# Second mixture: another order of the seven block products, copies ahead of casts on ScalarE, input forms over two rounds

## The chip, the cores and the metric

The kernel runs on one core of a Trainium2 chip. The time is the device time of one execution in microseconds (us), the median of the runs. PE is the matrix engine (TensorE), ACT is ScalarE, DVE is VectorE, POOL is GpSimd, SP issues the weight loads. Each engine works through a stream of instructions of its own, and semaphores order them against each other.

## What is computed

Attention over a window of 128 keys (4 batches, 8 heads, 576 positions), then a mixture of 8 experts with one expert for each token, then the second mixture, which this change is about: 4 experts on all 2304 tokens, weighted by given probabilities.

```python
def _moe2_ref(x, domain_probs, w1, w2):          # x 2304x512, w1 4x512x1024, w2 4x1024x512
    p = domain_probs / (domain_probs.sum(-1, keepdims=True) + 1e-09)
    out = np.zeros((N, D), dtype=np.float32)
    for e in range(E):
        h = np.maximum(x @ w1[e], 0.0)
        out += p[:, e:e + 1] * (h @ w2[e])
    return out
```

## The kernel before

Every fp32 matrix is carried as two fp32r tiles, an upper one (a cast on ACT) and a lower one (what the cast left, a subtraction on DVE); a product is three matmuls (upper by upper, upper by lower, lower by upper). The order of all instructions is written out by hand: each engine works through its own instructions in the order in which the program names them.

The second mixture runs 24 units, `unit2(u)`: 3 passes over the tokens (768 tokens each, two chunks of 384), 4 experts each, 2 rounds each (half of the hidden columns). So units 0, 8 and 16 are the first of a pass, units 7, 15 and 23 the last.

**Layer 1 of a unit** multiplies a 2x2 block matrix of the weights by one of the inputs with seven block products instead of eight. The inputs' seven *forms* are made once in a pass by `x_forms`, a generator that makes one form for each `next`: `b11`, `b21` and `b22` are plain blocks (one cast on ACT, one subtraction on DVE), `t1` to `t4` are differences (one subtraction `less` on DVE ahead of that). A product goes into two PSUM banks, twelve matmuls in all, by `step(banks, weight form, input form, start)`. There are three pairs of banks. `X` goes on accumulating over four products (a11, s2, s3, a22), and its sums on the way are needed: `keep` copies the two X banks on ACT after a11 (`m1`), after s2 (`u2`) and after s3 (`u3`). The next product into X may start only when the bank has been copied. `join` adds a copy to a bank of Y or Z on DVE and makes the upper half of the hidden tile with a Relu on ACT; `low` makes its lower half on DVE. The order of the products before: X a11, Z s1, X s2, X s3, Y a12, X a22, Z s4.

**Layer 2** has six accumulations (`n` = 0 to 5) of twelve matmuls, two banks of `ps_g` and one of `ps_t` in turn; `gather` adds each to the output rows on DVE (`acc`, line 1137). The last unit of a pass stores each row tile with an indirect DMA issued on POOL.

Between the steps `between(...)` advances generators: `ahead` prepares weight tiles (a tile of w2 is one 1024-wide cast on ACT and one subtraction `wlo` on DVE; a tile of w1 has its mixed forms besides), two advances in layer 1 (the w2 tiles of this same unit, here called item 2 and item 3) and four in layer 2 (items 0 and 1 of the next unit). `opening` is `x_forms(0)` in unit 0, where two forms had been made before; `closing` is `x_forms(p + 1)` in the last unit of a pass, which makes all seven forms of the next pass, three in layer 1 and four in layer 2.

Of the kernel before, what the change touches and what calls it, by code (L numbers as in the profile page):

```python
# [26 lines left out]
E1, E2 = 8, 4  # L27
# [3 lines left out]
NPASS = NCHUNK // 2  # L31
# [16 lines left out]
def kernel(  # L48
# [582 lines left out]
    def moe():  # L631
        mctx = ExitStack()
        with mctx:
# [15 lines left out]
            def form(n, name):  # L649
                pool = xp if n < 2 * NDT else late_forms[0]  # L650
                return pool.tile([P, 2, CH], F32R, tag=f"f{n}", name=name)
# [35 lines left out]
            def x_forms(p):  # L687
                l, r = (slice((2 * p + k) * CH, (2 * p + k + 1) * CH) for k in range(2))
                (b11, b12), (b21, b22) = ((x2[j][:, :, l], x2[j][:, :, r]) for j in range(2))
                now = ready[p] = {}  # L690

                temp = x2[0][:, :, N:]

                def split(n, k, src):
                    hi, lo = (form(2 * n + i, f"{k}{'hl'[i]}{p}") for i in range(2))
                    nc.scalar.copy(out=hi, in_=src)
                    nc.vector.tensor_tensor(out=lo, in0=src, in1=hi.bitcast(F32), op=ALU.subtract)
                    now[k] = hi, lo

                def less(out, a, b):  # L700
                    nc.vector.tensor_tensor(out=out, in0=a, in1=b, op=ALU.subtract)  # L701

                split(0, "b11", b11)
                yield
                less(temp, b12, b11)
                split(1, "t1", temp)
                yield
                less(temp, b22, temp)
                split(2, "t2", temp)
                yield  # L710
                less(b12, b22, b12)
                split(3, "t3", b12)
                yield
                split(4, "b21", b21)
                yield
                less(temp, b21, temp)
                split(5, "t4", temp)
                yield
                split(6, "b22", b22)
                yield  # L720

            def first_mixture():
                pctx = ExitStack()
                with pctx:
# [257 lines left out]
                    for _ in post:  # L982
                        pass

            forms = x_forms(0)

            def early(n):
# [18 lines left out]
            accs = {}  # L1006
            rounds = [(p, e, r) for p in range(NPASS) for e in range(E2) for r in range(2)]

            def unit2(u):
                p, e, r = rounds[u]  # L1010
                opening = forms if u == 0 else iter(())
                closing = x_forms(p + 1) if (e, r) == (E2 - 1, 1) and p + 1 < NPASS else iter(())
                w0 = n_first + ROUND * u
                xf = ready[p]
                at = {
                    "a11": (0, 0), "a12": (0, Q), "a22": (0, 2 * Q), "s3": (0, 3 * Q),
                    "s1": (2, 0), "s2": (2, Q), "s4": (2, 2 * Q),
                }

                def product(ps, n, a, b, start):  # L1020
                    tile0, c0 = at[a]
                    whi, wlo = wts[n][tile0:tile0 + 2]
                    xhi, xlo = xf[b]
                    for kt in range(2):
                        for x, (wl, xl) in enumerate(((whi, xhi), (whi, xlo), (wlo, xhi))):
                            nc.tensor.matmul(  # L1026
                                ps, wl[:, c0 + kt * P:c0 + (kt + 1) * P], xl[:, kt, :],
                                start=(start and kt == 0 and x == 0), stop=(kt == 1 and x == 2),
                                skip_group_check=not start,
                            )  # L1030

                def bank(tag, nm):
                    pool = {"a": ps_a, "g": ps_g, "t": ps_t}[tag]
                    return pool.tile([P, CH], F32, tag=tag, name=nm)

                xb, yb = ([bank("a", f"{k}{u}_{i}") for i in range(2)] for k in "XY")
                zb = [bank("g", f"Z{u}_{i}") for i in range(2)]
                hs = {}
                snaps = {}

                def keep(k, i):
                    if u == 0:
                        to = yp.tile([P, DM], F32, tag="y", name=f"{k}_{i}")[:, 0:CH]
                    else:
                        j, d = {"m1": (0, 1), "u2": (1, 0), "u3": (1, 1)}[k]
                        to = x2[j][:, d, (2 * p + i) * CH:(2 * p + i + 1) * CH]
                    nc.scalar.copy(out=to, in_=xb[i])  # L1047
                    snaps[k, i] = to

                def join(key, k, ps):  # L1050
                    hi = hp_.tile([P, CH], F32R, tag="hhi", name="hhi")
                    lo = hp_.tile([P, CH], F32R, tag="hlo", name="hlo")
                    c = ps
                    if k is not None:
                        c = sums[k[1]]
                        nc.vector.tensor_tensor(out=c, in0=ps, in1=snaps.pop(k), op=ALU.add)  # L1056
                    nc.scalar.activation(out=hi, in_=c, func=AF.Relu)  # L1057
                    hs[key] = hi, lo, c

                def low(key):  # L1060
                    hi, lo, c = hs[key]
                    nc.vector.scalar_tensor_tensor(  # L1062
                        out=lo, in0=c, scalar=0.0, in1=hi.bitcast(F32), op0=ALU.max, op1=ALU.subtract
                    )

                def step(bs, a, b, start):
                    for i in range(2):
                        product(bs[i], w0 + i, a, b, start)

                def between(*more):  # L1070
                    next(opening, None)
                    for todo in more:
                        next(todo, None)

                step(xb, "a11", "b11", True)
                between(ahead)
                for i in range(2):
                    keep("m1", i)
                step(zb, "s1", "t1", True)
                between(ahead, closing)  # L1080
                step(xb, "s2", "t2", False)
                between(closing)
                for i in range(2):
                    keep("u2", i)
                step(xb, "s3", "t3", False)
                between(closing)
                for i in range(2):
                    keep("u3", i)
                for i in range(2):
                    join((1, 1, i), ("u3", i), zb[i])  # L1090
                step(yb, "a12", "b21", True)
                between()
                for i in range(2):
                    low((1, 1, i))
                for i in range(2):
                    join((0, 0, i), ("m1", i), yb[i])
                step(xb, "a22", "t4", False)
                for i in range(2):
                    low((0, 0, i))
                for i in range(2):  # L1100
                    join((1, 0, i), None, xb[i])
                step(zb, "s4", "b22", False)
                for i in range(2):
                    low((1, 0, i))
                for i in range(2):
                    join((0, 1, i), ("u2", i), zb[i])
                for i in range(2):
                    low((0, 1, i))

                for n in range(2 * TT):  # L1110
                    k, t = divmod(n, TT)
                    acc = (ps_g, ps_t)[n % 2].tile([P, DM], F32, tag="gt"[n % 2], name="l2")
                    ts = slice(t * P, (t + 1) * P)
                    order = [(h, i) for h in ((0, 1), (1, 0))[k] for i in range(2)]
                    for m, (h, i) in enumerate(order):
                        whi, wlo = wts[w0 + 2 + h]
                        hhi, hlo, _ = hs[h, k, i]
                        c0 = i * DM
                        for x, (hl, wl) in enumerate(((hhi, whi), (hhi, wlo), (hlo, whi))):
                            nc.tensor.matmul(  # L1120
                                acc, hl[:, ts], wl[:, c0:c0 + DM],
                                start=(m == 0 and x == 0), stop=(m == 3 and x == 2),
                            )
                    if n < 4:
                        next(ahead, None)
                    if n > 1:
                        next(closing, None)
                    gather(p, e, r, n, acc)

# [19 lines left out]
    with tc.manual_schedule():  # L1149
        attention()  # L1150
        moe()
# [58 lines left out]
```

## Time and profile before

| | |
|---|---|
| three runs | 1201.73, 1202.87, 1203.39 us; median 1202.87 |
| the profiled execution | 1197.88 us; span from first to last instruction 1196.2 us |
| PE, ACT, DVE busy | 1167.6, 517.7, 785.6 us of the span |
| second mixture | from 431.8 us to the end |

Most of the second mixture is PE work without gaps, so what is to be looked for is how long single units last, and where PE sat idle in the longer ones. A row of the timeline gives the start of an instruction, its duration, engine and line, the tiles that it writes and reads, and in brackets the idle time of its engine ahead of it with what ended that.

### The profile page before, as it was taken

To read this page: it belongs to the slowest core of one execution; us is meant where nothing else is said; L and a number is where in the kernel's file an instruction comes from. 1 tells how busy PE (TensorE), PEld (TensorE's weight loads), DVE (VectorE), ACT (ScalarE), POOL (GpSimd) and SP (SyncE) were. 2 spreads that over 40 slices of the span, in tenths; PEclk is the share of its full clock that TensorE was granted. 3 is DMA by queue.
4 is the path that set the end of the run, shared out by engine and by line. 5 is a ranking of instruction groups with operands and counts; after the bars stand their busy time and mean duration, and the time that the engine had idled before them with its cause. 6 is when DMAs were issued, how large, how long until landed. Compare 5 with 4: busy or idle time off the path is not lost.

```text
span 1196.2 us, 18240 instructions
## 1 busy us (share of the span) xinstructions
PE 1167.6 (98%) x7006; PEld 1061.4 (89%) x7006; DVE 785.6 (66%) x1434; ACT 517.7 (43%) x926; POOL 94.7 (8%) x127
## 2 busy tenths in 40 slices
PE   8999998999999999999999899999999999999997
PEld 6888877999999988999999799999998899999996
DVE  6878764555565467666667876666667766666663
ACT  4565542454454344333334444443334433333331
POOL 8300110012200000000000110000000200000001
PEclk9999999999999999999999999999999999999999
DMA  9755424464574322222222222222221322222201
GB/s 315 262 163 188 142 63 155 143 200 141 159 221 149 124 72 71 71 71 71 65 63 67 89 88 69 57 69 71 71 65 58 124 72 71 71 71 71 71 19 53
DMA packets 62232, 126.67 MB, mean 106 GB/s; under 512 B 26272, under 2 KB 26272, under 8 KB 62112
## 3 DMA queue, kind: packets, MB, share of 16 engines
q1 hardware_dynamic: 58368, 114.96, 30.7%
q0 software_dynamic: 3456, 9.51, 2.1%
q8 instruction: 83, 1.36, 0.5%
q10 hardware_dynamic: 288, 0.52, 0.1%
q14 instruction: 37, 0.30, 0.1%
HBM read 109.18 MB, written 15.80 MB: 104 GB/s over the span
## 4 chain that ended last, share of the span: by engine, by line
issue 42%; PE 37%; DVE 2%; POOL 2%; ACT 1%; POOLq 0%; ACTq 0%; DVEq 0%
PE g L679 10%; PE l L1120 9%; PE y L786 8%; PE X L1026 4%; PE Z L1026 2%; POOL out_dram L1141 2%; PE y L797 1%; PE Y L1026 1%; PE xps L742 1%; DVE hlo L1062 1%; DVE x L701 0%; ACT hhi L1057 0%; DVE x L1056 0%; ACT whi L126 0%; PE g L767 0%
## 5 line engine op out<-in xcount | busy, mean ns | idle before, releaser
L130 DVE TENSOR_TENSOR wlo<-raw,whi 128x1024 fp32r<-128x1024 f32 x160 | 195.0, 1221 | 113.4 <-ACT whi L126 113.3
L1120 PE MATMUL l<-whi,hhi 128*128 128x512 f32 x576 | 225.4, 391 | 4.3 <-DVE acc L1137 4.0
L126 ACT CAST whi<-raw 128x1024 fp32r<-128x1024 f32 x160 | 168.3, 1057 | 134.1 <-DVE raw L152 104.6
L1120 PE MATMUL l<-whi,hlo 128*128 128x512 f32 x576 | 225.6, 392 | 0.0
L1120 PE MATMUL l<-wlo,hhi 128*128 128x512 f32 x576 | 225.3, 391 | 0.0
L1047 ACT COPY x<-X 128x384 f32<-128x384 f32 x138 | 65.8, 480 | 237.7 <-PE X L1026 237.7
L1137 DVE SCALAR_TENSOR_TENSOR acc<-l,ct,acc 128x512 f32<-128x512 f32 x126 | 94.3, 749 | 82.2 <-PE l L1120 82.2
L1120 PEld LDWEIGHTS l<-whi,hhi 128*128 128x128 f32 x576 | 108.6, 189 | 27.5 <-DVE acc L1137 4.8
L1120 PEld LDWEIGHTS l<-whi,hlo 128*128 128x128 f32 x576 | 108.5, 188 | 22.9 <-DVE hlo L1062 0.3
L1120 PEld LDWEIGHTS l<-wlo,hhi 128*128 128x128 f32 x576 | 108.6, 189 | 22.0
L1057 ACT ACTIVATE hhi<-x 128x384 fp32r<-128x384 f32 x144 | 74.1, 526 | 75.0 <-DVE x L1056 75.0
L1056 DVE TENSOR_TENSOR x<-Z,x 128x384 f32<-128x384 f32 x92 | 50.8, 556 | 81.9 <-ACT x L1047 72.9
L1141 POOL DMA_INDIRECT out_dram<-acc,ctok x18 | 23.0, 1276 | 842.9 <-DVE acc L1137 493.2
L1062 DVE SCALAR_TENSOR_TENSOR hlo<-x,hhi 128x384 fp32r<-128x384 f32 x144 | 77.4, 554 | 11.5 <-ACT hhi L1057 7.5
L400 ACT ACTIVATE pr<-sc,nm 128x256 f32<-128x256 f32 (+1 forms) x144 | 58.9, 464 | 52.4 <-DVE nm L392 24.6
L426 PE MATMUL xo<-vr,ptr 128*128 128x73 f32 x544 | 69.0, 279 | 0.6 <-ACT ptr L413 0.5
L786 PE MATMUL y<-hhi,whi 128*128 128x256 f32 (+2 forms) x224 | 69.5, 310 | 0.0
L786 PE MATMUL y<-hhi,wlo 128*128 128x256 f32 (+2 forms) x224 | 69.1, 308 | 0.0
L786 PE MATMUL y<-hlo,whi 128*128 128x256 f32 (+2 forms) x224 | 68.9, 308 | 0.0
L426 PEld LDWEIGHTS xo<-vr,ptr 128*128 128x128 f32 x544 | 63.7, 192 | 5.8 <-ACT ptr L413 1.3
L667 DVE SCALAR_TENSOR_TENSOR hlo<-g,hhi 128x384 fp32r<-128x384 f32 x64 | 32.7, 552 | 29.8 <-ACT hhi L666 29.5
L666 ACT ACTIVATE hhi<-g 128x384 fp32r<-128x384 f32 x64 | 28.0, 489 | 54.5 <-PE g L767 41.7
(337 smaller groups left out, 2546.4 us busy)
## 6 DMA issues: line engine op xcount, KB each, us to landing
raw<-in_w_b_dram SPq DMA_DIRECT2D x96, 512.0 KB, 3.5
raw<-in_w_a_dram SPq DMA_DIRECT2D x64, 512.0 KB, 4.1
xs<-zrow SPq DMA_DIRECT2D x8, 768.0 KB, 6.9
row<-xs SPq DMA_DIRECT2D x7, 768.0 KB, 5.6
rk<-in_k_dram SPq DMA_DIRECT2D x18, 256.0 KB, 4.9
vr<-in_v_dram SPq DMA_DIRECT2D x18, 256.0 KB, 3.9
rv<-in_vt_dram SPq DMA_DIRECT2D x18, 256.0 KB, 3.4
rq<-in_q_dram SPq DMA_DIRECT2D x16, 256.0 KB, 5.2
```

The source lines that it names most:

```text
L126: nc.scalar.copy(out=hi, in_=src)
L130: nc.vector.tensor_tensor(out=lo, in0=src, in1=hi.bitcast(F32), op=ALU.subtract)
L400: nc.scalar.activation(out=pr[:, r, jj, 0:w], in_=sc[s][:, r, jj, 0:w], func=AF.Exp, bias=nm[:, r, jj:jj + 1], scale=1.0,)
L426: nc.tensor.matmul(xo[:, 2 * jj + r, :], pt[:, r, c, :], vr[:, keys[c] % NSLOT, h, :], start=(c == 0), stop=(c == nk - 1),)
L679: nc.tensor.matmul(ps[:, 0:w], wl[:, c0:c0 + P], xl[dt // 2][:, dt % 2, 0:w], start=(n == 0), stop=(n == 3 * NDT - 1),)
L786: nc.tensor.matmul(acc[:, 0:w], wl[:, c0:c0 + P], hl[:, 0:w], start=(f == 0 and x == 0), stop=(f == NFT - 1 and x == 2),)
L1026: nc.tensor.matmul(ps, wl[:, c0 + kt * P:c0 + (kt + 1) * P], xl[:, kt, :], start=(start and kt == 0 and x == 0), stop=(kt == 1 and x == 2) ...
L1047: nc.scalar.copy(out=to, in_=xb[i])
L1057: nc.scalar.activation(out=hi, in_=c, func=AF.Relu)
L1062: nc.vector.scalar_tensor_tensor(out=lo, in0=c, scalar=0.0, in1=hi.bitcast(F32), op0=ALU.max, op1=ALU.subtract)
L1120: nc.tensor.matmul(acc, hl[:, ts], wl[:, c0:c0 + DM], start=(m == 0 and x == 0), stop=(m == 3 and x == 2),)
L1137: nc.vector.scalar_tensor_tensor(out=accs[g], in0=acc, scalar=pe, in1=accs[g], op0=ALU.mult, op1=ALU.add)
```

## The change

- **Order of the products.** After: X a11, Z s1, Y a12, X s2, X s3, X a22, Z s4. Y a12 stands two steps earlier, and X s2, s3 and a22 follow each other directly.
- **Copies ahead of casts.** `keep("m1")` is issued ahead of `between(ahead)`, no longer behind it. Behind X s2 and X s3 no `between` stands any more; the copies are issued right behind their products. The join of the block (0, 0), from Y and `m1`, is issued behind Y a12, that is ahead of the copies of `u2`.
- **Forms over two rounds.** `b21` is made third instead of fifth. The last unit of a pass makes five forms of the next pass (two in layer 1, three in layer 2, at `n` = 2, 4, 5) and leaves `t4` and `b22` to the first unit of the next pass, which makes them in its first two `between`. Unit 0 makes `b21` and `t2` ahead of its first product, and `t3`, `t4`, `b22` in its three `between`.
- **Where copies go.** The first unit of every pass, not only unit 0, keeps its copies in the pool `yp`, in which the output rows live too.

```diff
 def x_forms(p):
                 split(1, "t1", temp)
                 yield
+                split(2, "b21", b21)
+                yield
                 less(temp, b22, temp)
-                split(2, "t2", temp)
+                split(3, "t2", temp)
                 yield
                 less(b12, b22, b12)
-                split(3, "t3", b12)
-                yield
-                split(4, "b21", b21)
+                split(4, "t3", b12)
                 yield
...
+            border = {0: forms}
+
             def unit2(u):
                 p, e, r = rounds[u]
-                opening = forms if u == 0 else iter(())
-                closing = x_forms(p + 1) if (e, r) == (E2 - 1, 1) and p + 1 < NPASS else iter(())
+                fresh = (e, r) == (0, 0)
+                opening = border.pop(p) if fresh else iter(())
+                closing = iter(())
+                if (e, r) == (E2 - 1, 1) and p + 1 < NPASS:
+                    closing = border[p + 1] = x_forms(p + 1)
...
                 def keep(k, i):
-                    if u == 0:
+                    if fresh:
...
+                def pair(do, *a):                    # do(*a, i) for i in 0, 1
+                def joined(h, k, kept, bs):          # join for i in 0, 1
+                def lows(h, k):                      # low for i in 0, 1
+                if u == 0:
+                    next(opening)
+                    next(opening)
                 step(xb, "a11", "b11", True)
+                pair(keep, "m1")
                 between(ahead)
-                for i in range(2):
-                    keep("m1", i)
                 step(zb, "s1", "t1", True)
                 between(ahead, closing)
+                step(yb, "a12", "b21", True)
+                joined(0, 0, "m1", yb)
+                between(closing)
                 step(xb, "s2", "t2", False)
-                between(closing)
-                for i in range(2):
-                    keep("u2", i)
+                pair(keep, "u2")
+                lows(0, 0)
                 step(xb, "s3", "t3", False)
-                between(closing)
-                for i in range(2):
-                    keep("u3", i)
-                for i in range(2):
-                    join((1, 1, i), ("u3", i), zb[i])
-                step(yb, "a12", "b21", True)
-                between()
-                for i in range(2):
-                    low((1, 1, i))
-                for i in range(2):
-                    join((0, 0, i), ("m1", i), yb[i])
+                pair(keep, "u3")
+                joined(1, 1, "u3", zb)
                 step(xb, "a22", "t4", False)
-                for i in range(2):
-                    low((0, 0, i))
-                for i in range(2):
-                    join((1, 0, i), None, xb[i])
+                lows(1, 1)
+                joined(1, 0, None, xb)
                 step(zb, "s4", "b22", False)
...
-                    if n > 1:
+                    if n in (2, 4, 5):
                         next(closing, None)
                     gather(p, e, r, n, acc)
```

## Rows read from the trace of the kernel before

**Rows 1.** Busy time of each engine in units 0, 4, 7, 8, 15.

```profile
core 0: us, PE busy (x) PEld busy (x) DVE busy (x) ACT busy (x) POOL busy (x), PEclk, DMA share, GB/s
431.79:466.62 34.83, 32.08 (x159) 27.88 (x158) 26.99 (x41) 16.85 (x27) 0.00 (x0) 1.00 0.22 73
...
559.46:590.40 30.94, 30.94 (x157) 28.11 (x156) 20.72 (x34) 12.16 (x20) 0.00 (x0) 1.00 0.23 68
652.30:689.10 36.80, 33.12 (x157) 29.15 (x156) 30.33 (x45) 17.17 (x27) 6.11 (x5) 0.95 0.27 86
689.10:720.05 30.95, 30.95 (x158) 28.11 (x156) 20.82 (x34) 12.23 (x20) 2.30 (x2) 1.00 0.27 86
905.73:940.97 35.24, 31.56 (x158) 28.01 (x156) 29.01 (x44) 16.69 (x27) 5.81 (x4) 1.00 0.28 90
```

**Rows 2.** Waits of PE, the whole span: us in total, times, longest.

```profile
PE l L1120 <- DVE acc L1137: 4.0, 2, 2.0
PE X L1026 <- ACT x L1047: 3.4, 2, 1.7
```

**Rows 3.** Timeline of unit 0 (starts at 431.79): DVE, ACT and one PE row.

```profile
432.49 0.96 DVE L701 TENSOR_TENSOR x<-x,x 128x768 f32<-128x768 f32 x1 [1.32 <-ACT x L834]
433.48 0.83 ACT L696 CAST t2h<-x 128x768 fp32r<-128x768 f32 x1 [1.02 <-DVE x L701]
434.35 0.96 DVE L697 TENSOR_TENSOR t2l<-x,t2h 128x768 fp32r<-128x768 f32 x1 [0.90 <-ACT t2h L696]
...
438.17 1.04 ACT L126 CAST whi<-raw 128x1024 fp32r<-128x1024 f32 x1
439.11 0.83 ACT L696 CAST b21h<-x 128x768 fp32r<-128x768 f32 x1
439.24 1.23 DVE L130 TENSOR_TENSOR wlo<-raw,whi 128x1024 fp32r<-128x1024 f32 x1
439.85 0.85 ACT L1047 COPY u<-X 128x384 f32<-128x384 f32 x2
440.37 0.44 PE L1026 MATMUL X<-t3h,whi 128*128 128x384 f32 x1 [2.09 <-ACT u L1047]
440.38 0.95 DVE L697 TENSOR_TENSOR b21l<-x,b21h 128x768 fp32r<-128x768 f32 x1
441.25 0.95 DVE L701 TENSOR_TENSOR x<-x,x 128x768 f32<-128x768 f32 x1
```

**Rows 4.** Timeline of unit 4 (starts at 559.46): PE, ACT and DVE.

```profile
561.82 0.48 ACT L1047 COPY x<-X 128x384 f32<-128x384 f32 x1 [0.56 <-PE X L1026]
562.19 1.05 ACT L126 CAST whi<-raw 128x1024 fp32r<-128x1024 f32 x1
...
564.68 0.33 PE L1026 MATMUL X<-t2h,shi 128*128 128x384 f32 x1
564.93 0.48 ACT L1047 COPY x<-X 128x384 f32<-128x384 f32 x1 [1.69 <-PE X L1026]
565.72 0.33 PE L1026 MATMUL X<-t3h,whi 128*128 128x384 f32 x1
...
570.20 1.02 DVE L1056 TENSOR_TENSOR x<-Y,x 128x384 f32<-128x384 f32 x2
570.84 0.99 ACT L1057 ACTIVATE hhi<-x 128x384 fp32r<-128x384 f32 x2 [1.15 <-DVE x L1056]
```

**Rows 5.** PE in one microsecond behind unit 7's wait in layer 2: busy time, granted clock.

```profile
686.00:687.00 1.00, 1.00 (x4) 0.50 0.32 131
```

**Rows 6.** Timeline of unit 7, layer 2: the DVE and PE rows around accumulation n = 5.

```profile
683.86 0.75 DVE L1137 SCALAR_TENSOR_TENSOR acc<-l,ct,acc 128x512 f32<-128x512 f32 x1
684.52 0.95 DVE L701 TENSOR_TENSOR x<-x,x 128x768 f32<-128x768 f32 x1
...
684.66 0.50 PE L1120 MATMUL l<-whi,hhi 128*128 128x512 f32 x1 [1.98 <-DVE acc L1137]
```

**Rows 7.** The 18 indirect stores of output rows, line 1141: issue to landing.

```profile
DMA to landing us min/median/max: 2.7/3.7/5.7
```

More of the change, by code (lines that the diff above doesn't have):

```diff
@@ L1073, in between @@
                         next(todo, None)
+                def pair(do, *a):
+                    for i in range(2):
+                        do(*a, i)
+                def joined(h, k, kept, bs):
+                    for i in range(2):
+                        join((h, k, i), kept and (kept, i), bs[i])
+                def lows(h, k):
+                    for i in range(2):
+                        low((h, k, i))
+                if u == 0:
+                    next(opening)
+                    next(opening)
                 step(xb, "a11", "b11", True)
+                pair(keep, "m1")
                 between(ahead)
-                for i in range(2):
-                    keep("m1", i)
                 step(zb, "s1", "t1", True)
                 between(ahead, closing)
+                step(yb, "a12", "b21", True)
+                joined(0, 0, "m1", yb)
+                between(closing)
                 step(xb, "s2", "t2", False)
-                between(closing)
-                for i in range(2):
-                    keep("u2", i)
+                pair(keep, "u2")
+                lows(0, 0)
                 step(xb, "s3", "t3", False)
-                between(closing)
-                for i in range(2):
-                    keep("u3", i)
-                for i in range(2):
-                    join((1, 1, i), ("u3", i), zb[i])
-                step(yb, "a12", "b21", True)
-                between()
-                for i in range(2):
-                    low((1, 1, i))
-                for i in range(2):
-                    join((0, 0, i), ("m1", i), yb[i])
+                pair(keep, "u3")
+                joined(1, 1, "u3", zb)
                 step(xb, "a22", "t4", False)
-                for i in range(2):
-                    low((0, 0, i))
-                for i in range(2):
-                    join((1, 0, i), None, xb[i])
+                lows(1, 1)
+                joined(1, 0, None, xb)
                 step(zb, "s4", "b22", False)
[L1103 to L1108, printed above, removed]
+                lows(1, 0)
+                joined(0, 1, "u2", zb)
+                lows(0, 1)
                 for n in range(2 * TT):
```

## The prediction

> **What bounds the kernel now.** I first cut the second mixture into its 24 units and read the busy time of the engines in each [rows 1]. An ordinary unit lasts 30.94 us and PE is busy for all of it; DVE has 20.7 us of work and ACT 12.2. There the order of the steps can gain nothing. Only three units are longer: unit 0 (34.83), unit 7 (36.80) and unit 15 (35.24), by 3.89 + 5.86 + 4.30 = 14.05 us. That is all that this change can take away.
>
> Then I read what PE waits for [rows 2]. In units 7 and 15 it waits twice: for a copy of X, 1.7 us each, and in layer 2 for the gather of an earlier accumulation, 2.0 us each. In unit 0 it waits 2.09 us for the copy of u2 [rows 3]; the rest there is smaller waits for b22's lower half and a gather, and slow first matmuls behind a wait (0.44 instead of 0.33 us, so 0.1 each) [rows 3, 4]. Unit 7 is 1.56 longer than unit 15, because behind the same wait the granted clock fell to its lower level (0.50, which is 1.2 of 2.4 GHz) [rows 5].
>
> **How a unit is followed by hand.** T is the start of its first product. A bank's product takes 1.04 us (t2's second bank at 564.68, t3's first at 565.72) [rows 4], a step 2.08. In both orders X s2 is directly in front of X s3. After the change it is the fourth step, so X s3 is due at T+8.33, and it can start only when bank 0 has been copied: copy u2 on ACT starts 0.25 behind the bank's end (564.68 to 564.93) [rows 4], takes 0.48, and PE starts 0.04 later. So the copy may start at T+7.53 and has to by T+7.81: 0.27 us of play. What matters is what ACT has in its stream in front of that copy. Before, in an ordinary unit: nothing. After: the two Relus of the join (0, 0), which wait for two adds on DVE, which stand behind all that DVE was given in the first three steps.
>
> Prices, as start to start when nothing waits: copy 0.37 (561.82 to 562.19), add 0.46, Relu 0.46 (pairs of 1.02 and 0.99) [rows 4]; 1024-wide cast 0.94, 768-wide cast 0.74 (439.11 to 439.85), wlo 1.13, lower half of a form 0.87 (440.38 to 441.25) [rows 3]; acc 0.66 [rows 6]. A hand-over between ACT and DVE costs 0.03 to 0.04. A difference form is a round trip: less 0.96, cast 0.83, lower half 0.87, two hand-overs: 2.73 us in which DVE gets nothing else done [rows 3].
>
> **The 19 ordinary units.** Second copy of m1 at T+2.33; item 2's cast at 2.70 to 3.75 (before, with no copies in front, it could run in layer 2 of the unit before); wlo at 3.79 and 4.92; adds at 6.05 and 6.52 to 7.08; second Relu at 7.11; copy u2 at 7.57, PE could go on at 8.09, due 8.33. It holds, with 0.24 us to spare: cost 0. The copies of u3 now have X a22 directly behind them, but nothing in front of them on ACT: 9.62 to 10.10, due 10.41, cost 0. The hidden tiles for layer 2 come as before, behind X a22 and Z s4.
>
> **Unit 0** (T = 431.79, X s3 due at 440.12). b21's cast starts when the first mixture's last copy ends, 432.46 (it released DVE's less at 432.49) [rows 3]. Its lower half runs 433.33, then DVE is free at 434.20; t2 2.73: 436.93; t3 2.73: 439.66. Item 2's cast stands behind t3's (437.92 + 0.74), ends 439.71, wlo to 440.88. t4: 443.61. Item 3's cast stands behind t4's (442.61), ends 443.66, wlo to 444.83. Adds of the join at 444.83 and 445.30, second Relu at 445.89, then b22's cast (its `between` precedes the copies) at 446.35, copy u2 at 447.09 to 447.57. X s3 at 447.6: 7.5 late, with the slow first matmul 7.6. No other wait is left, since DVE catches up meanwhile: 3.89 become 7.6.
>
> **Units 7 and 15.** Layer 1: wlo to 6.05, b11's lower half 0.87, adds 6.92 and 7.39, t1's less at 7.86, its cast at 8.85, copy u2 at 9.59 to 10.07, PE at 10.11: 1.8 late, which is what it is now. Layer 2: gather 3, for which accumulation 5 waits, was 2.13 late; now t3's round trip is behind it, but b21's cast queues behind item 1's two casts and holds gather 2 back. I take 0.75 left, bounds 0 and 2.1. With two slow starts 2.75 each.
>
> **Units 8 and 16**, which lose nothing now (30.95) [rows 1]. Gather 3 ends 0.04 before accumulation 5, that is at T-2.86; t2 and its round trip follow, gather 4 at T-0.2, t3 at 0.44 to 3.17, gather 5 to 3.83, t4's less 3.83, its lower half 5.69 to 6.56. Item 2's cast behind t4's: 5.56 to 6.61; wlo 6.65 to 7.78; b22's lower half to 8.65; item 3's wlo to 9.78; adds 9.78 and 10.25; second Relu 10.84; copy u2 11.30 to 11.78. X s3 at 11.82 instead of 8.33: 3.5 late, 3.6 each. So the stall at the border of passes is not spread thin but moved to where the join stands in front of the copy.
>
> **Edits at no cost.** Copies of units 8 and 16 in `yp` wait for stores of the pass before: the last one is issued about T+4 and lands 3.7 us later, at most 5.7 [rows 7], its buffer is wanted by the second u3 copy at T+10.65 or later. Weight loads leave SP behind item 2's and item 3's wlo, which end by T+6.1 now; the tiles they fetch are wanted in layer 2, behind T+14.6. POOL's own queue is unchanged.
>
> **Sum.** After: 7.6 + 2 x 2.75 + 2 x 3.6 = 20.3; before 14.05: +6.25 us with no clock lost. Clock: of five waits of 1.7 to 2.1 us in this stage one was followed by the lower level, at 1.56 [rows 1, 5]. The three new ones are longer (7.5, 3.5, 3.5) than any of these; I count the fall fully for the first and half for the others: 3.1 (bounds 0 and 4.7). Together +9.35: 1207.2 beside the profiled 1197.88, and on the median 1202.87, which is 5 us above that execution for reasons that the trace cannot show, 1212.2.
>
> **Rivals.**
>
> *The clock falls each time.* All three new waits are followed by the lower level, at 1.56 each: +6.25 + 4.7 = +10.95, 1213.8. For it: each is longer than the longest wait seen. Against: four of the five shorter ones show no fall. Chance 0.25. The Trainium skill (TensorE: Matmul & The Clock Gate, "Part 1: The HAM clock gate") says that the throttled level is the default and that sustained idleness brings it back; that is this case, and the one fall seen behind 2 us agrees with it, the other four waits do not show it.
>
> *Play eaten in ordinary units.* If DVE and ACT overlapped less than in these pairs, each wlo (1.23 instead of 1.13), add and Relu would come 0.1 later, 0.37 in all against 0.24: a wait of 0.12 and a slow start 0.1 in 19 units, +4.2, 1216.4. It decides from 0.24. Against it: all rows that follow each other overlap [rows 3, 4]. Chance 0.13. The Trainium skill (VectorE: DVE Perf Modes, "The DRAIN you can't avoid") states that the next VectorE operation waits until the pipe is empty; the pair of adds here, 1.02 for two of 0.56, does not show it.
>
> *The moved forms are hidden.* The join reaches ACT in time in units 8 and 16, if DVE's backlog from unit 7 is 3.5 us shorter than I add up; then -7.2 and -1.6 of clock: 1203.4, no change. Chance 0.08. For it: DVE is busy 30.3 of 36.8 us in unit 7, so not all of it is full.
>
> *Faster.* The opposite sign needs unit 0's chain too: if ACT got to u2's copy by 439.6, that is if the round trips of b21, t2, t3, t4 cost DVE no more than their own work, the stalls of 0, 8 and 16 vanish and the layer-2 waits shrink: 14.05 - 5.5 = 8.5 less, 1194.4. For it: PE's present waits are just those that the copies and forms cause [rows 2]. Against: the round trips stand in the rows [rows 3]. Chance 0.08.
>
> **Numbers.** The forecast has 0.46, the rivals 0.25, 0.13, 0.08 and 0.08; the first three cases are all slower by far more than 0.2% (2.4 us, about what a measurement of this kernel tells from no change). Low end: +6.25, less 1.7 for no wait in layer 2 and 2 for the hand sums: 1205. High end: all clock falls, layer 2's wait unchanged and the ordinary units' play eaten: 6.25 + 4.7 + 2.7 + 4.2 = 17.9, 1220.7. Slower 0.84, same 0.08, faster 0.08.
>
> **What would show it.** In the changed profile units 0, 8 and 16 would last 38 to 40, 34.5 to 36 and again 34.5 to 36 us, with PE waiting for u2's copy in front of X s3, ACT's Relus waiting for DVE's adds, and the adds directly behind a wlo. Units 7 and 15 would have 33.7. Ordinary units would stay at 30.94; 31.1 or more shows the play eaten. Wrong would be the forecast if units 8 and 16 stayed under 32, or if unit 0 got shorter than 34.8.

## The result, and the profile after

The changed kernel takes 1213.53 us (median of 6 runs, 1211.49 to 1214.31), the kernel before, beside it, 1201.46: a ratio of 1.01, 95% interval 1.0083 to 1.0117. It is 12.1 us slower.

The busy time of the engines in the units of the changed kernel that answer to those of before [rows 1], and one ordinary unit (the second row, unit 3):

```profile
core 0: us, PE busy (x) PEld busy (x) DVE busy (x) ACT busy (x) POOL busy (x), PEclk, DMA share, GB/s
436.51:476.88 40.37, 33.07 (x158) 29.95 (x158) 27.48 (x41) 16.33 (x26) 0.00 (x0) 0.92 0.19 63
538.78:569.72 30.94, 30.94 (x157) 28.10 (x156) 20.77 (x34) 12.15 (x20) 0.00 (x0) 1.00 0.21 68
662.56:696.56 34.00, 31.52 (x157) 27.98 (x156) 25.45 (x40) 15.20 (x24) 5.28 (x4) 1.00 0.29 90
696.56:732.66 36.10, 32.84 (x158) 29.67 (x156) 25.81 (x40) 14.25 (x23) 2.87 (x2) 0.95 0.22 76
918.34:952.34 34.00, 31.52 (x158) 27.99 (x156) 25.46 (x40) 15.20 (x24) 5.81 (x4) 1.00 0.30 91
952.34:988.40 36.06, 32.79 (x157) 29.64 (x156) 25.80 (x40) 14.26 (x23) 2.87 (x2) 0.95 0.23 76
```

Units 0, 7, 8, 15, 16 together went from 168.76 to 180.53 us, +11.8: this is nearly all of the 12.1. Units 7 and 15 got shorter (36.80 and 35.24 to 34.00), units 0, 8 and 16 longer by 5.5, 5.15 and 5.1, and in these the granted clock is below 1. Ordinary units are the same. The profiled spans differ by more, 16.4, because unit 0 starts 4.7 us later in this execution; no instruction ahead of unit 0 has changed, and in the profiles below it starts anywhere from 433.6 to 440.2. Two profiles of one kernel (the seventh run and its repeat) differ by 1.66 us in this start and by 1.72 in their time. The profiled execution of before starts earliest of all; that this is why it lay 5 us under its runs is likely, but one profile can't show it.

PE's waits in the changed kernel, as [rows 2] (the columns are us in total, times, longest):

```profile
PE X L1031 <- issue: 7.3, 1, 7.3
PE X L1031 <- ACT u L1052: 6.5, 2, 3.3
PE X L1031 <- ACT x L1052: 3.4, 2, 1.7
...
PE l L1127 <- DVE acc L1144: 1.6, 2, 0.8
```

The wait of unit 0 carries the name "issue": this view found no releaser for it. The timeline shows it. To be set beside [rows 3], the timeline of unit 0 of the changed kernel, first the rows of ACT:

```profile
437.21 0.84 ACT L696 CAST b21h<-x 128x768 fp32r<-128x768 f32 x1
439.94 0.84 ACT L696 CAST t2h<-x 128x768 fp32r<-128x768 f32 x1 [1.89 <-DVE x L701]
...
447.40 1.04 ACT L126 CAST whi<-raw 128x1024 fp32r<-128x1024 f32 x1
450.20 0.99 ACT L1062 ACTIVATE hhi<-x 128x384 fp32r<-128x384 f32 x2 [1.76 <-DVE x L1061]
451.09 0.81 ACT L696 CAST b22h<-x 128x768 fp32r<-128x768 f32 x1
451.81 0.85 ACT L1052 COPY u<-X 128x384 f32<-128x384 f32 x2
```

The rows of DVE in the same timeline, at the join:

```profile
448.47 1.22 DVE L130 TENSOR_TENSOR wlo<-raw,whi 128x1024 fp32r<-128x1024 f32 x1
449.61 1.01 DVE L1061 TENSOR_TENSOR x<-Y,m 128x384 f32<-128x384 f32 x2
```

And PE's, where the wait ends:

```profile
452.38 0.66 PE L1031 MATMUL X<-t3h,whi 128*128 128x384 f32 x1 [7.30 <-issue]
452.84 0.52 PE L1031 MATMUL X<-t3l,whi 128*128 128x384 f32 x1
```

Read backwards from X s3: it starts at 452.38, 0.09 behind the end of the first copy of u2 (451.81 + 0.48). That copy stands behind b22's cast and the two Relus; the Relus waited 1.76 us for the adds of the join; the adds stand directly behind item 3's wlo, whose cast ended at 448.44. The first matmul takes 0.66 and the next 0.52 instead of 0.33: PE runs at the lower clock when the wait is over, as this stretch of unit 0 shows (PE's busy time, granted clock 0.50, then DMA), to be set beside [rows 5]:

```profile
453.00:455.00 2.00, 2.00 (x8) 0.50 0.03 8
```

In unit 8 (start 696.56) the same chain, DVE's rows:

```profile
693.57 0.95 DVE L701 TENSOR_TENSOR x<-x,x 128x768 f32<-128x768 f32 x1
695.42 0.96 DVE L697 TENSOR_TENSOR t2l<-x,t2h 128x768 fp32r<-128x768 f32 x1 [0.90 <-ACT t2h L696]
696.29 0.75 DVE L1144 SCALAR_TENSOR_TENSOR acc<-l,ct,acc 128x512 f32<-128x512 f32 x1
...
700.34 0.95 DVE L701 TENSOR_TENSOR x<-x,x 128x768 f32<-128x768 f32 x1
702.19 0.96 DVE L697 TENSOR_TENSOR t4l<-x,t4h 128x768 fp32r<-128x768 f32 x1 [0.90 <-ACT t4h L696]
703.14 1.23 DVE L130 TENSOR_TENSOR wlo<-raw,whi 128x1024 fp32r<-128x1024 f32 x1
704.28 0.95 DVE L697 TENSOR_TENSOR b22l<-x,b22h 128x768 fp32r<-128x768 f32 x1
705.16 1.22 DVE L130 TENSOR_TENSOR wlo<-raw,whi 128x1024 fp32r<-128x1024 f32 x1
706.29 1.01 DVE L1061 TENSOR_TENSOR x<-Y,m 128x384 f32<-128x384 f32 x2
```

The idle time of 0.90 in front of a form's lower half is the round trip: the next instruction in DVE's own stream is that lower half, so DVE idles while ACT casts. The adds start at T+9.73; the hand sum had 9.78.

### The profile page after: what moved, and what is told of

Its sections match the earlier page's. It is cut to its first block, busy times and chain, and to the rows that moved or that the text cites. A ratio compares the mean times of both kernels' runs of the same rounds, so it can differ in the third digit from the quotient of the medians.

```text
span 1212.6 us, 18215 instructions
## 1 busy us (share of the span) xinstructions
PE 1172.9 (97%) x7006; PEld 1067.2 (88%) x7006; DVE 787.9 (65%) x1434; ACT 518.1 (43%) x926; POOL 92.6 (8%) x127
## 4 chain that ended last, share of the span: by engine, by line
issue 42%; PE 39%; POOL 2%; DVE 1%; ACT 0%; POOLq 0%; DVEq 0%; ACTq 0%
PE g L679 10%; PE l L1127 9%; PE y L786 8%; PE X L1031 6%; PE Z L1031 3%; POOL out_dram L1148 2%; PE y L797 1%; PE Y L1031 1%; PE xps L742 1%; PE g L767 0%; DVE x L1061 0%; DVE wlo L130 0%; POOLq L1213 0%; PE y L767 0%; ACT x L1052 0%
## 5 line engine op out<-in xcount | busy, mean ns | idle before, releaser
L1052 ACT COPY x<-X 128x384 f32<-128x384 f32 x126 | 59.9, 477 | 217.6 <-PE X L1031 217.6
L1061 DVE TENSOR_TENSOR x<-Z,x 128x384 f32<-128x384 f32 x84 | 46.8, 557 | 55.6 <-ACT x L1052 45.5
```

## The experiments

All runs change only the second mixture. Their units, in us (ordinary units 30.94 to 30.97 but in the fifth run), so that each can be read against the others; a number behind the time is the ratio to the kernel before, run beside it on the same chip, with its 95% interval:

| run | time, ratio | unit 0 | 7 | 8 | 15 | 16 |
|---|---|---|---|---|---|---|
| before | 1201.46 | 34.83 | 36.80 | 30.95 | 35.24 | 30.94 |
| changed | 1213.53, 1.0100 (1.0083 to 1.0117) | 40.37 | 34.00 | 36.10 | 34.00 | 36.06 |
| e1_copy_first | 1202.51, 0.9988 (0.9968 to 1.0009) | 36.83 | 33.20 | 32.44 | 33.21 | 32.43 |
| e2_less_ahead | 1205.08, 1.0018 (0.9997 to 1.0040) | 37.31 | 34.45 | 32.43 | 34.49 | 32.43 |
| e3_filled_waits | 1208.56, 1.0038 (1.0020 to 1.0056) | 38.55 | 34.06 | 34.48 | 34.03 | 34.51 |
| e4_both | 1193.86, 0.9921 (0.9890 to 0.9952) | 32.56 | 33.24 | 30.95 | 33.20 | 30.97 |
| e5_more_relu | 1221.54, 1.0153 (1.0132 to 1.0173) | 40.89 | 34.03 | 37.30 | 34.01 | 36.05 |
| e6_all_seven | 1216.13, 1.0116 (1.0093 to 1.0138) | 41.02 | 40.05 | 31.00 | 39.79 | 30.94 |
| e7_no_waits | 1192.15, 0.9908 (0.9888 to 0.9929) | 32.37 | 31.96 | 30.95 | 31.97 | 30.95 |
| e8_after_join | 1190.78, 0.9905 (0.9884 to 0.9925) | 32.39 | 30.97 | 31.05 | 30.97 | 31.05 |

The changed kernel was not run again beside these kernels. The kernel before, which was, came out at 1201.46, 1203.32, 1203.19 and 1202.25 us in the four sets, so a difference of two times out of different sets is good to about 2 us. The units of the profiled executions are the surer measure, and both are given.

**The join behind the copies.** The changed kernel with one move:

```diff
                 step(yb, "a12", "b21", True)
-                joined(0, 0, "m1", yb)
-                between(closing)
                 step(xb, "s2", "t2", False)
                 pair(keep, "u2")
+                joined(0, 0, "m1", yb)
+                between(closing)
                 lows(0, 0)
```

> The changed kernel with one move: the join of block (0, 0) and the between in front of it are issued behind the copies of u2. Theory (the join in ScalarE's stream holds the copy back): the wait in front of X s3 goes to 4.0 us in unit 0 (what is left is item 3's cast behind two round trips), to 0 in units 7 and 15, to 0.4 in units 8 and 16; the copies of u3 get 1.3, 0.7 and 0.9 in their place, and accumulation 5 in units 7 and 15 waits 1.2. Waits together 12.8 instead of 20.3 us, the lower clock gone behind units 8 and 16: about -10.5 against the changed kernel, 1203. Rival (the place of the join is of no account, the casts of the forms hold the copy): units 8 and 16 stay at 36 us, 1213.

1202.51, 11 us less than the changed kernel; the five units together 12.4 less. The waits of PE in this kernel:

```profile
PE X L1031 <- issue: 3.8, 1, 3.8
...
PE l L1127 <- DVE acc L1144: 2.4, 2, 1.2
...
PE X L1031 <- ACT u L1052: 1.5, 2, 0.8
```

In units 8 and 16 X s3 starts 0.31 us later than in step, where it was 3.4 late, with a wait of 0.8 for u3 in its place; in unit 0 the wait is 3.8, what the casts of t3, t4 and item 3 still hold back. So the place of the join was the cause at the borders, and nearly half of the wait in unit 0, where b22's cast moved along with it.

**The difference of the next form issued ahead.** `x_forms` of the changed kernel rewritten so that `less` of the next form precedes the lower half of the present one, wherever the next form's temporary allows it (the comments explain; they are not in the kernel):

```diff
...
-                split(2, "b21", b21)
-                yield
-                less(temp, b22, temp)
-                split(3, "t2", temp)
+                ahead_of(2, "b21", b21, (temp, b22, temp))   # cast b21; less of t2; lower half of b21
+                yield
+                ahead_of(3, "t2", temp, (b12, b22, b12))     # cast t2; less of t3; lower half of t2
...
```

> The changed kernel with one change in x_forms: the difference of the next form is issued on VectorE ahead of the lower half of the form before, so that VectorE doesn't idle through the cast. Theory (the round trips of 2.73 us are what makes the chain in front of the join long): the wait for the copy of u2 goes from 7.5 to 3.5 us in unit 0, from 3.4 to 1.4 in units 8 and 16, and to 2.2 (no better) in units 7 and 15; together 12.9 instead of 20.2, and the lower clock gone behind units 8 and 16: about -10, 1203. Rival (VectorE is simply full there): the waits stay within 0.5 us of now, 1213.

1205.08, 8.5 less; the units together 9.4 less. PE's waits for u2, and DVE's rows in unit 0 (line 708 is the lower half here):

```profile
PE X L1035 <- issue: 3.4, 1, 3.4
...
PE X L1035 <- ACT u L1056: 2.4, 2, 1.2
```

```profile
440.30 0.95 DVE L708 TENSOR_TENSOR t3l<-x,t3h 128x768 fp32r<-128x768 f32 x1
441.17 1.22 DVE L130 TENSOR_TENSOR wlo<-raw,whi 128x1024 fp32r<-128x1024 f32 x1
442.31 0.95 DVE L708 TENSOR_TENSOR t4l<-x,t4h 128x768 fp32r<-128x768 f32 x1
```

The idle time in front of the lower halves of t3 and t4 is gone. Units 8 and 16 are 32.43, and X s3 was 3.55 late in unit 0 instead of 7.47. Units 7 and 15 got 0.45 longer, as expected. So DVE was not full: it stood idle for the round trips. The run missed the expected 1203 by 2 us; the waits are those expected, but behind the wait of unit 0 the lower clock cost 2.7 us here instead of 1.9.

**Waits filled with matmuls.** Behind X s2 in units 0, 8 and 16 PE multiplies zeros into a spare bank:

```diff
                 step(xb, "s2", "t2", False)
+                if fresh:
+                    busy(ps_t, "t", 30 if u == 0 else 13)
```

> The changed kernel with bf16 matmuls of zeros into a spare PSUM bank behind X s2: 30 in unit 0, 13 in units 8 and 16, so that PE works through nearly all of its wait. Theory (the three falls of the clock follow from the waits and cost 1.6 each): units 0, 8 and 16 get 1.6 us shorter each, with the granted clock at 1.00 behind the wait, 4.7 together: about 1208.8. Rival (the clock falls at these places whatever PE does, or its cost is part of the wait): no change, 1213.5.

1208.56, 5.0 less than the changed kernel; units 0, 8, 16 shorter by 1.8, 1.6 and 1.55. In unit 8 the timeline of PE shows the filler and then matmuls at full speed:

```profile
703.02 2.98 PE L97 MATMUL idle<-idle 128*128 128x512 bf16 x12
706.41 0.44 PE L1031 MATMUL X<-t3h,whi 128*128 128x384 f32 x1 [0.41 <-ACT u L1052]
706.69 0.34 PE L1031 MATMUL X<-t3l,whi 128*128 128x384 f32 x1
```

PE's busy time there, and the granted clock of 1.00:

```profile
706.50:708.50 2.00, 2.00 (x12) 1.00 0.43 162
```

X s3 starts at T+11.74, where it was T+11.78 in the changed kernel, and still the unit is 1.6 us shorter: the fall of the clock is a cost of its own, on top of the wait.

**Both moves.** The first two edits together.

> The changed kernel with both moves of the two runs before: copies of u2 ahead of the join, and the difference of the next form one form ahead. Theory: waits of 1.4 us in unit 0 (copy of u3), 0.7 and 1.2 in units 7 and 15, none in units 8 and 16; 5.8 together, no fall of the clock: 20 us less than the changed kernel, about 1194, and 7 to 8 less than the kernel before. Rival (either move alone gets all there is): 1203, as the kernel before.

1193.86, as the theory had it: 19.7 us less than the changed kernel, where the moves alone gave 11.0 and 8.5. By the units it is 19.6 together and 12.4 and 9.4 alone. They nearly add up; each alone already saves the falls of the clock in units 8 and 16. PE waits 1.4 in unit 0 and 0.65 and 1.34 in units 7 and 15, starts to starts over the usual step, nowhere else, and the clock does not fall. Unit 0, columns as in the first table of units:

```profile
435.14:467.70 32.56, 31.31 (x159) 28.14 (x158) 26.64 (x41) 16.21 (x26) 0.00 (x0) 1.00 0.21 65
```

**One Relu more in ordinary units.**

```diff
                 joined(0, 0, "m1", yb)
+                if not fresh and (e, r) != (E2 - 1, 1):
+                    more = hp_.tile([P, CH], F32R, tag="hhi", name="more")
+                    nc.scalar.activation(out=more, in_=xf["b21"][0][:, 0, :].bitcast(F32), func=AF.Relu)
```

> The changed kernel with one Relu more (384 wide, into a tile that nobody reads) on ScalarE behind the join of block (0, 0), in the 19 ordinary units alone. Theory (0.24 us to spare in front of X s3): the Relu takes 0.46, PE waits 0.22 and starts slowly 0.1 later: ordinary units of 31.2 to 31.3 instead of 30.95, +6 us together, 1219.6. Rival (the copy of u2 has much more play than the hand sum says, since the ordinary units of the changed kernel show no wait): ordinary units stay at 30.95, 1213.5.

Ordinary units are 31.23 to 31.30. (Unit 23 has no extra Relu by this edit and stays as it was, so 18 units got one, not 19.) In the timeline of one of them, unit 2, X s3 starts 0.34 behind the matmul ahead of it instead of 0.17, and its first matmul takes 0.44:

```profile
517.16 0.34 PE L1031 MATMUL X<-t2h,slo 128*128 128x384 f32 x1
517.50 0.44 PE L1031 MATMUL X<-t3h,whi 128*128 128x384 f32 x1
```

The copy of u2 in unit 2, in the changed kernel (the unit starts at 507.83) and in this one (508.99):

```profile
515.47 0.46 ACT L1052 COPY x<-X 128x384 f32<-128x384 f32 x1
```

```profile
516.99 1.08 ACT L1052 COPY x<-X 128x384 f32<-128x384 f32 x2
```

It starts at T+7.64 and at T+8.00. The Relu moved it by 0.36, of which 0.17 came out as a wait; so the play in the ordinary units is real and small, about 0.2 us, less than one more operation on ACT. The total is 2 us over the expected 1219.6. Against the kernel before, on its own chip, it is 18.35 us slower where the changed kernel is 12.07, that is 6.3 more, about what was expected. In the profiled execution units 0 and 8 came out longer too, with the same waits: the lower clock held on longer. Unit 8:

```profile
699.24:736.54 37.30, 34.04 (x158) 30.87 (x156) 25.80 (x40) 14.39 (x23) 2.88 (x2) 0.91 0.22 73
```

**All seven forms in the last unit of a pass.**

```diff
-                    if n in (2, 4, 5):
+                    if n > 0:
                         next(closing, None)
```

> The changed kernel with all seven forms of the next pass made in the last unit of a pass again (five in its layer 2, at n = 1 to 5), none left to the first unit of the next. Theory (the work on VectorE and ScalarE stays, only the place of the wait goes with it): units 8 and 16 go from 36.1 to 30.95, units 7 and 15 wait for gather 3 some 4.4 us instead of 0.8 and get 37.6 or, with the lower clock, 39: sum the same within 2 us, 1213. Rival (leaving forms to the next round is what costs): units 8 and 16 go to 30.95 and units 7 and 15 stay at 34, -10 us, 1203.

1216.13. Units 8 and 16 are ordinary again, and units 7 and 15 wait 4.4 for the gather, as PE's waits show:

```profile
PE l L1127 <- DVE acc L1144: 8.8, 2, 4.4
```

They grow by 6, more than units 8 and 16 gain (5.1), for this wait too was followed by the lower clock. Unit 7:

```profile
661.24:701.29 40.05, 33.97 (x158) 29.77 (x156) 30.36 (x45) 17.50 (x27) 6.71 (x5) 0.92 0.25 79
```

The wait is the expected 4.4, but the units are 1 to 2 us longer than the expected 37.6 or 39. So spreading the forms over two rounds is not what cost. Units 7, 8, 15 and 16 together take 141.8 us here and 140.2 in the changed kernel, but that is the clock: the waits of a pair of units (7 and 8) are 6.4 and 6.25 us, and the lower clock cost 2.5 and 2.2 here against 1.6 and 1.6, lengths that differ from one execution to the next. A gain by the spreading is not shown. With these round trips the wait only changes its place.

**No waits.** Both moves; the `between` behind the copies of u3; and accumulations 3 and 5 of layer 2 in banks of X and Y:

```diff
                 pair(keep, "u3")
+                between(closing)
                 joined(1, 1, "u3", zb)
...
-                    acc = (ps_g, ps_t)[n % 2].tile([P, DM], F32, tag="gt"[n % 2], name="l2")
+                    pool, tag = ((ps_g, "g"), (ps_t, "t"), (ps_a, "a"))[(0, 1, 0, 2, 0, 2)[n]]
+                    acc = pool.tile([P, DM], F32, tag=tag, name="l2")
```

> The two moves of the fourth run (copies of u2 ahead of the join, differences one form ahead), the between behind the copies of u3, and accumulations 3 and 5 of layer 2 in banks of X and Y, free by then, so that they don't wait for gathers 1 and 3. Theory: all waits gone but 0.7 us for the copy of u3 in unit 0: units 7, 8, 15 and 16 at 30.95, unit 0 at 31.8: 5 us less than the fourth run, 1189. Rival (VectorE falls behind by what it doesn't wait for, and the first unit of the next pass waits instead): units 8 and 16 get 1 to 2 us longer, 1192.

1192.15, and 1192.44 when it ran again beside the next run: a miss by 3 us. PE's waits, from which those for gathers are gone (and the rival's wait in units 8 and 16 did not come), hold one that I had not counted:

```profile
PE Z L1035 <- DVE x L1065: 1.7, 3, 0.7
```

Z s4 accumulates on the banks that the join (1, 1) reads; the work of a form on DVE (t1 in units 7 and 15, b22 in unit 0) now stood in front of its adds.

**The form behind the join.** The kernel of the seventh run with:

```diff
                 pair(keep, "u3")
-                between(closing)
+                if u == 0:
+                    between()
                 joined(1, 1, "u3", zb)
+                between(closing)
```

> The seventh run with one move: outside unit 0 the between that makes t1 stands behind the join of block (1, 1), no longer in front of it. Theory (in the seventh run the form's work on VectorE stood in front of the adds that free the Z banks, and Z s4 waited 0.9 us in units 7 and 15): units 7 and 15 at 30.95 to 31.1 instead of 31.96, unit 0 unchanged at 32.4: -2 us, 1190. Rival (VectorE is full in these units, so the wait only goes on to layer 2): units 7 and 15 stay near 32, 1192.

> The seventh run again, beside the eighth on the same chip: 1192.

1190.78 beside 1192.44, ranges that overlap; by the units it is 1.8 us less. Units 7 and 15 are ordinary now. Busy time of the engines in unit 0, then 7 and 8 of this kernel, columns as above:

```profile
433.62:466.01 32.39, 31.57 (x158) 28.11 (x158) 26.75 (x41) 16.24 (x26) 0.00 (x0) 1.00 0.22 65
651.82:682.78 30.96, 30.96 (x158) 28.05 (x156) 24.55 (x39) 14.79 (x24) 3.92 (x4) 1.00 0.25 71
682.78:713.83 31.05, 31.05 (x158) 28.05 (x157) 26.20 (x41) 14.58 (x23) 4.24 (x3) 1.00 0.35 117
```

This beats both kernels, the one before by 11.5 us (0.95%, run beside it) and the changed one by 22.8 us (from another set), with the changed kernel's order of products. 1.6 us of the 14.05 that could be had are left, in units 0, 8 and 16.

## Why the prediction was right

The cause was followed by hand ahead of the run, and the traces bear it out; one term was too small, and one was partly lucky.

- **Unit 0.** X s3 7.5 late by the hand sum; idle of 7.30 before it, 7.47 from start to start over the usual step. The chain in the trace is the one written down, link by link: the copy of u2 starts at T+15.30 in both.
- **Units 8 and 16.** 3.5; measured 3.43 and 3.44. E1 and e6 show that the join in front of the copy and the two forms left over make this wait together: without either it is gone.
- **Units 7 and 15.** 1.8 and 0.75 for the two waits; 1.86 and 0.96, starts to starts over the usual step. The 0.75 was chosen between the bounds 0 and 2.1 and not followed by hand, so its closeness is in part luck.
- **Ordinary units.** 0.24 us to spare and cost 0: 30.94 to 30.95. The copy came 0.07 later than the hand sum has it (T+7.64 for T+7.57), and the trace and e5 put the play at about 0.2.
- **Edits at no cost.** Nothing in units 8 and 16 waits for the stores or the weight loads; the copies of u2 there start as soon as the Relus are done, those of u3 as soon as the product is. Neither the pool `yp` nor the earlier place of the `m1` copies was tried alone.
- **The clock** is the term that was mis-sized. I took 3.1 us (one fall and two halves); all three waits were followed by the lower level, and the falls cost 1.9 + 1.6 + 1.6 (5.05 unrounded), what units 0, 8 and 16 lost beyond their waits and slow starts of 0.1; e3 gave 5.0 back when it filled the waits. With 5.0 in place of 3.1 the sum would be +11.3; the units show +11.8, the runs +12.1. The rival "the clock falls each time" (1213.8, chance 0.25) is what happened, on top of the forecast's waits. For the same reason the units lie a little above the signs given for them: 40.37 for 38 to 40 in unit 0, 36.10 and 36.06 for 34.5 to 36.
- **The time is closer than the change.** 1212.2 is 1.3 us under the measured time, but +9.35 is 2.7 under the measured +12.1. The difference is the kernel before, 1202.87 in three runs then and 1201.46 in six now: 1.4 us of luck.

Of the other rivals, the play was not eaten (e5 shows what that looks like), and the moved forms were not hidden. That the opposite sign needs the cost of the round trips gone, as that rival has it, was borne out by e2 and e4: with `less` one form ahead and the copy in front of the join the same order is faster than before.

## What to carry over

Where an engine works through its stream in order, ask of every copy that frees a bank what stands ahead of it in that stream, and what those instructions wait for on other engines; a cast that waits for a subtraction delays everything behind it. A chain that goes to and fro between two engines is shortened by issuing the first half of the next link before the second half of the present one. And before moving work to another place, add up the engine that makes it: if it idles through hand-overs, the wait moves along with the work, as e6 shows.

## What the runs showed of the hardware

Waits of PE in units 0, 7, 8, 15 and 16 (before, changed, and the first six experiments, filled waits left out; starts to starts over the usual step): of 11 with 3.43 to 7.48 us all were followed by the lower clock, of 22 with 1.3 to 2.3 us one was. A fall cost from 1.6 us to 2.8 (unit 8 of the fifth run, 37.30 against 36.10 of the changed kernel with the same wait). Filling the waits of units 0, 8 and 16 with matmuls of zeros kept the clock at 1.00. The Trainium skill (TensorE: Matmul & The Clock Gate, "Part 1: The HAM clock gate") states that sustained idleness brings the throttled level back. These runs agree, and show besides one fall behind a wait of 2.13 us (1.98 of them idle, unit 7 of the kernel before).
